# Asking for the next head's K six tiles earlier in an attention loop

## The chip, the cores and the metric

The kernel runs on one core of one Trainium2 chip. The metric is the device time of one execution in microseconds; the time before is the median of three runs. A separate, profiled execution gave the trace from which all durations here are taken.

## The reference

A transformer block with modulation: one attention over a given K and V cache, then a small mixer and MLP. B = 1, S = 2048, D = 640, 32 heads of 128, all tensors bf16.

```python
def _A_ref(x, k_cache, v_cache, wq, wo):
    q = (x @ wq).reshape(B, Sq, H, Dh).transpose(0, 2, 1, 3)
    scores = einsum('bhqd,bhkd->bhqk', q, k_cache) * Dh ** (-0.5)
    p = softmax(scores, axis=-1)
    o = einsum('bhqk,bhkd->bhqd', p, v_cache)
    return o.transpose(0, 2, 1, 3).reshape(B, Sq, H * Dh) @ wo
...
mod = (silu(c) @ w_mod)                      # sa, ca, ga, sb, cb, gb
h = layernorm(x) * (1 + ca) + sa
x = x + ga * _A_ref(h, k_cache, v_cache, wq, wo)
h = layernorm(x) * (1 + cb) + sb
return x + gb * _B_ref(h, w1, w2, w3, w4)    # shifted mixer and MLP
```

## The kernel before, in words

The kernel has three stages. The first loads x and the modulation weights, normalizes x and forms its transpose hT. The second, four fifths of the time, is attention. The third does the output projection, the mixer and the MLP.

**Attention** is one loop over steps s. Step s takes query tile j = s % 16 (128 queries) of head h = s // 16, so there are 512 tiles. For each tile:

1. TensorE computes the scores of 128 queries against 2048 keys into PSUM (qk, L297, tile Sps, in two halves of 1024 columns).
2. VectorE (DVE) reads each half once: it writes the scaled, negated scores to SBUF and takes the row minimum on the way (L570, tile negS). negS has three buffers, so DVE can be at most three tiles ahead of ScalarE.
3. GpSimd (POOL) joins the two minima (L580), and ScalarE (ACT) takes the exponential into one of eight buffers Pb (L583; eight RPB slots of the tile ring).
4. The probabilities must be transposed for the second product. For 15 of 16 tiles this is a transposing DMA from Pb to PTs, one of twelve RPT slots of the same tile ring (L234, "ring<-ring"). It is issued from SP, two tiles at a time: pairs (0,1), (2,3), (4,5), (6,7), (8,9), then tile 10 alone, then (12,13) and (14,15). Tile 11 is transposed by TensorE instead (t_piece, L264) and copied out by ACT (L273).
5. TensorE multiplies the transposed tile by V (pv, L310, tile PTp), eleven steps after the scores of that tile (PVD = 11; the lag falls to 8 in the last head). The product carries a column of ones, which gives the row sums. ACT copies it to Of (L561), POOL divides (L458) and stores four tiles at a time to a DRAM scratch tensor o_scratch (L465), on POOL's DMA queue.

Between these, TensorE computes the queries of head h+1 in pieces (q_piece, L248), which ACT copies out (L255).

**Loads.** K, transposed by the DMA on its way in (load_k, L207), and V (load_v, L226) have two buffers each, for even and odd heads. Heads 0 and 1 get their K ahead of the loop. At step j = 11 of a head (PVD) SP is given the K and the V of the next head, and in every fourth head a part of Wo (load_wo, L217). V can't be asked for earlier, since PV of the head before reads its buffer eleven steps behind the scores. K's buffer is read by qk only, and so is free once the last tile of the head before has its scores.

**Order.** Every engine runs its own list in the order in which the program adds operations, and waits for semaphores where an operation needs another engine's result. SP's list is a single queue too: a transposition waits on SP for the exponential of its second tile, and everything behind it on SP waits as well. K of head h+1 stands in SP's list behind the single transposition of tile 10, which stands behind that of tiles 8 and 9.

Of the kernel before, what the change touches and what calls it, by code (L numbers as in the profile page):

```python
# [115 lines left out]
def bass_adaLN_cond__mha_block_cached__mixer_s_mlp__prompt_kernel(  # L116
# [3 lines left out]
    _, H, SK, DH = A_k_cache.shape  # L120
# [17 lines left out]
    with ExitStack() as es:  # L138
# [11 lines left out]
        if True:  # L150
            with ExitStack() as es1:
# [53 lines left out]
                def load_k(h):  # L205
                    hb = h % 2
                    G.dma("sync", lambda e: e.dma_start_transpose(KTs[:, hb], A_k_cache[0, h]), ("k", hb), w=[("KT", hb)])  # L207
# [24 lines left out]
                def transpose(g, n):  # L232
                    b, t = g % RPB, g % RPT
                    G.dma("sync", lambda e: e.dma_start_transpose(  # L234
                        PTs[:, t:t + n].rearrange("p r k q -> p (r k) q"), ring[:, b:b + n].rearrange("p r s -> p (r s)")),
                        ("t", b), r=[("Pb", b + i) for i in range(n)], w=[("PT", t + i, z) for i in range(n) for z in range(2)])
# [9 lines left out]
                def q_piece(h, cc, q):  # L246
                    jb = bank(("q", h, cc))
                    G.op("tensor", lambda t: t.matmul(JB[jb], wqg[:, h // WG, q, (h % WG) * 128:(h % WG + 1) * 128], hT[:, q, cc * 512:(cc + 1) * 512],  # L248
                                                      start=(q == 0), stop=(q == KT - 1)),
                         r=[("wq", h), ("hT", cc, q)], w=[("J", jb)])  # L250
# [39 lines left out]
                def qk(s, half):  # L290
                    h, j = divmod(s, NQT)
                    hb = h % 2

                    def f(t):
                        for c2 in range(2):
                            col = half * 1024 + c2 * 512
                            ins = t.matmul(Sps[:, col:col + 512], QT[:, hb, j * 128:(j + 1) * 128],  # L297
                                           KTs[:, hb, col:col + 512], start=True, stop=True)
                        return ins
                    G.op("tensor", f, r=[("QT", hb, j // 4), ("KT", hb)],  # L300
                         w=[("S", half)] + ([("Sb", 2 * half), ("Sb", 2 * half + 1)] if s == 0 else []))
# [110 lines left out]
                def q_head0(cc):  # L412
                    for q in range(KT):
                        q_piece(0, cc, q)
                    q_evac(0, cc)
# [22 lines left out]
                def mod_rows(i):  # L438
                    n0, n1 = MROW[i]
                    bank = PO[:, (i % 2) * 512:(i % 2) * 512 + n1 - n0]  # L440

                    def f(t):
                        for k in range(KT):
                            ins = t.matmul(bank, s_bc[:, k, :], wmodr[:, k, n0:n1], start=(k == 0), stop=(k == KT - 1))
                        return ins
                    G.op("tensor", f, r=[("sbc", k) for k in range(KT)] + [("wm", 1)] + WRK, w=[("O", i % 2)])
                    G.op("scalar", lambda a: a.copy(mod_bc[:, n0:n1], bank), r=[("O", i % 2)], w=[("mod", i)])
# [79 lines left out]
                for s in range(at[-1] + LAG + 1):  # L527
                    h, j = divmod(s, NQT)
                    pvs = PVS.get(s, [])
                    evacs = []  # L530
                    if s <= 2:
                        for i in ((0,), (1, 2), range(3, len(MROW)))[s]:
                            mod_rows(i)
                    if s == 3:
                        G.op("gpsimd", lambda g: g.tensor_scalar(
                            out=mod_bc[:, 2 * D:3 * D], in0=mod_bc[:, 2 * D:3 * D], scalar1=1.0, scalar2=1.0, op0=ALU.add, op1=ALU.mult),
                            r=[("mod", i) for i in range(len(MROW))], w=["mod"])
                    for half in range(2):
                        if s < NG:
                            qk(s, half)  # L540
                        for g_ in pvs:
                            if len(pvs) == 1:
                                pv(g_, half)
                            elif g_ == pvs[half]:
                                pv(g_, 0)
                                pv(g_, 1)
                        if s == 0 and half == 1:
                            q_head0(NQC - 1)
                        if h + 1 < H and 2 * j + half in QPIECE:
                            cc, q = QPIECE[2 * j + half]  # L550
                            q_piece(h + 1, cc, q)
                            if q == KT - 1:
                                evacs.append((q_evac, h + 1, cc))
                        for r, pt in [(r, pt) for r in range(2) for pt in PE_TILES]:
                            g = s - PE_LAG[pt] - r
                            if 0 <= g < NG and g % NQT == pt:
                                t_piece(g, r, half)
                                if half == 1:
                                    evacs.append((t_evac, g, r))
                    for p in [g_ // 2 for g_ in pvs if g_ % 2 == 1]:  # L560
                        G.op("scalar", lambda a, p=p: a.copy(  # L561
                            Of[:, p % 4].rearrange("p z d -> p (z d)")[:, 0:259], PO[:, (p % 2) * 512:(p % 2) * 512 + 259]),
                            r=[("O", p % 2)], w=[("Of", p % 4)])
                    for fn, x, y in evacs:
                        if fn is q_evac or not by_dve(x, y):
                            fn(x, y)
                    for half in range(2):
                        if s < NG:
                            r8 = s % 8
                            G.op("vector", lambda v, half=half, s=s, r8=r8: v.tensor_scalar(  # L570
                                out=negS[:, s % 3, half * 1024:(half + 1) * 1024],
                                in0=Sps[:, half * 1024:(half + 1) * 1024],
                                scalar1=-SCALE, scalar2=None, op0=ALU.mult, op1=ALU.min,
                                accum_out=(nm0 if half == 0 else nm1)[:, r8:r8 + 1]),
                                r=[("S", half)], w=[("negS", s % 3), ("nmh", half, r8)])
                    for fn, x, y in evacs:
                        if fn is t_evac and by_dve(x, y):
                            fn(x, y)
                    if s < NG:
                        G.op("gpsimd", lambda g, r8=r8: g.tensor_scalar(  # L580
                            out=nm[:, r8:r8 + 1], in0=nm0[:, r8:r8 + 1], scalar1=nm1[:, r8:r8 + 1], scalar2=None, op0=ALU.min),
                            r=[("nmh", 0, r8), ("nmh", 1, r8)], w=[("nm", r8)])
                        G.op("scalar", lambda a, s=s, r8=r8: a.activation(  # L583
                            Pb[:, s % RPB, :], negS[:, s % 3, :], ACT.Exp, bias=nm[:, r8:r8 + 1], scale=-1.0),
                            r=[("negS", s % 3), ("nm", r8)], w=[("Pb", s % RPB)])
                        if not is_pe(s):
                            if s % 2 == 1 and not is_pe(s - 1):
                                transpose(s - 1, 2)
                            elif s % 2 == 1 or is_pe(s + 1):
                                transpose(s, 1)  # L590
                        if j == PVD:
                            if 1 <= h < H - 1:
                                load_k(h + 1)
                            if h < H - 1:
                                load_v(h + 1)
                            if h % WG == WG - 1:
                                load_wo(h // WG)
                    for g_ in NORMS.get(s, []):
                        gr, z = divmod(g_, 4)
                        if z == 0:  # L600
                            rcp(gr)
                        norm(gr, z)
                    if s == OT0:
                        load_ot(0)
                        for cc in range(NQC):
                            load_xt(cc)
                    if s == OT0 + 1:
                        load_ot(1)
# [247 lines left out]
```

## Time and profile before

| | |
|---|---|
| Median of 3 runs | 1690.23 us (1686.36 to 1691.68) |
| Profiled execution | 1699.03 us, span 1697.2 us |
| Attention, first DVE pass of head 0 to last of head 31 | 35.3 to 1343.9 us |
| One DVE pass over 1024 columns (L570) | 1220 ns, 1024 of them |
| One exponential over 2048 columns (L583) | about 2.0 us, 512 of them |
| Granted TensorE clock, mean | 0.962 of full |

On the profile's page, busy times are shares of the span for each engine, and the digits of section 2 are the busy tenths of 40 equal slices. The DMA row counts the core's 16 DMA engines together. SP's rows in a timeline are DMA issues: a row lasts from when SP begins to issue the transfer to when it is through with it, and the landing comes after. The other engines' rows are instructions; a bracket behind a row gives the idle time just before it and what ended that.

### The profile page before, as it was taken

What the parts mean: (1) busy time and instruction counts of PE and PEld (TensorE: products, weight loads), DVE (VectorE), ACT (ScalarE), POOL (GpSimd) and SP (SyncE); (2) the same over time, 40 slices, a digit from 0 to 9 for tenths busy, and PEclk for the clock granted to TensorE, in tenths of its full rate; (3) what the DMA queues carried; (4) which work ended last, traced back from release to release, by engine and by line L of the source; (5) the groups of instructions that cost most, each with busy time, mean ns of one, the idle gap of its engine ahead of it and who ended that gap; (6) DMA issues with size and microseconds to landing.
All of it is one profiled execution on the core that took longest, in us unless ns stands there. A gap on an engine that the chain in (4) does not pass through costs nothing.

```text
span 1697.2 us, 33782 instructions
## 1 busy us (share of the span) xinstructions
PE 1505.5 (89%) x13474; PEld 968.5 (57%) x13719; DVE 1376.4 (81%) x2428; ACT 1282.6 (76%) x1113; POOL 622.8 (37%) x1394
## 2 busy tenths in 40 slices
PE   5898978988989899889888888988989889999998
PEld 3466656655666566556555555656656645555444
DVE  6998978988999899889888888988989636666424
ACT  4999978988999899889898998888989700035330
POOL 0244434443444344434443444444434523332100
PEclk8999989999999999999999999999999999999999
DMA  9999999999999999999999999999999995620000
GB/s 304 234 239 242 236 224 225 241 237 234 247 234 236 242 243 236 230 222 240 231 240 232 233 230 233 235 229 227 245 243 223 241 249 110 140 103 3 13 20 32
DMA packets 1218285, 350.32 MB, mean 206 GB/s; under 512 B 1193744, under 2 KB 1212112, under 8 KB 1218128
## 3 DMA queue, kind: packets, MB, share of 16 engines
q1 hardware_dynamic: 1211984, 331.36, 97.7%
q0 software_dynamic: 6144, 16.79, 3.7%
q8 instruction: 108, 1.77, 0.4%
q14 instruction: 49, 0.40, 0.1%
HBM read 43.48 MB, written 19.40 MB: 37 GB/s over the span
## 4 chain that ended last, share of the span: by engine, by line
DVE 48%; PE 24%; DMA 11%; issue 8%; ACT 7%; SPq 2%; POOL 1%; POOLq 0%
DVE negS L570 47%; DMA kv<-in_A_k_cache_dram 8%; PE Sps L643 7%; ACT ring L583 5%; PE Sps L784 4%; PE Sps L297 3%; PE PTp L310 2%; PE Oaug L768 2%; PE QPp L768 2%; SPq L234 2%; PE Sps L753 1%; PE QPp L264 1%; DMA ring<-in_A_x_dram 1%; DVE ring L375 1%; DMA negS<-o_scratch 1%
## 5 line engine op out<-in xcount | busy, mean ns | idle before, releaser
L570 DVE TENSOR_SCALAR_CACHE_REDUCE negS<-Sps 128x1024 f32<-128x1024 f32 x1024 | 1177.8, 1220 | 132.2 <-PE Sps L297 129.9
L583 ACT ACTIVATE ring<-negS,small 128x2048 bf16<-128x2048 f32 x512 | 1021.2, 2005 | 37.5 <-POOL small L580 35.0
L297 PE MATMUL Sps<-kv 128*128 128x512 bf16 x1962 | 611.9, 391 | 148.8 <-DMA kv<-in_A_k_cache_dram 101.1
L310 PEld LDWEIGHTS PTp<-kv,ring 128*128 128x128 bf16 x8192 | 574.3, 100 | 256.5 <-issue 22.5
L310 PE MATMUL PTp<-kv,ring 128*128 128x129 bf16 x8192 | 661.3, 224 | 6.0 <-DMA ring<-ring 4.7
L580 POOL TENSOR_SCALAR small<-small 128x1 f32<-128x1 f32 x512 | 145.9, 285 | 715.6 <-DVE negS L570 715.6
L297 PEld LDWEIGHTS Sps<-kv 128*128 128x128 bf16 x2048 | 146.3, 99 | 274.9 <-DVE negS L570 131.7
L458 POOL TENSOR_SCALAR On<-Of,small 128x128 bf16<-128x128 f32 x512 | 189.8, 371 | 15.4 <-DMA o_scratch<-On 2.4
L561 ACT COPY Of<-PTp 128x259 f32<-128x259 f32 x256 | 92.3, 360 | 95.1 <-PE PTp L310 95.0
L681 ACT COPY kv<-PTp 128x640 bf16<-128x640 bf16 x32 | 22.0, 692 | 154.9 <-PE PTp L678 154.9
L451 POOL TENSOR_TENSOR small<-Of,small 128x4 f32<-128x4 f32 x128 | 133.1, 1040 | 5.0 <-ACT Of L561 4.9
L465 POOL DMA_DIRECT2D o_scratch<-On x128 | 103.1, 806 | 40.8 <-POOL On L458 37.2
L248 PE MATMUL Oaug<-hTx,wo 128*128 128x512 bf16 x258 | 98.0, 385 | 2.9 <-DVE hTx L407 2.9
L248 PE MATMUL QPp<-hTx,wo 128*128 128x512 bf16 x260 | 98.1, 382 | 2.8 <-ACT hTx L402 2.3
L570 DVE DVE_READ_ACCUMULATOR negS<-Sps 128x1 f32 x1024 | 84.7, 83 | 0.0
L624 POOL TENSOR_SCALAR On<-On 128x1 f32<-128x1 f32 x48 | 24.3, 507 | 151.7 <-DVE On L633 151.7
L651 DVE TENSOR_TENSOR ring<-Sps,mod_bc 128x640 f32<-128x640 f32 x16 | 13.2, 824 | 78.3 <-PE Sps L643 78.3
L643 PE MATMUL Sps<-wo,hTx 128*128 128x128 bf16 (+1 forms) x504 | 71.0, 302 | 6.0 <-DMA hTx<-o_scratch 5.6
L643 PE MATMUL Sps<-wo,negS 128*128 128x128 bf16 (+1 forms) x504 | 69.1, 298 | 1.1 <-DMA negS<-o_scratch 0.7
L788 DVE TENSOR_TENSOR ring<-Sps,ring 128x640 f32<-128x640 f32 x16 | 13.2, 824 | 66.2 <-PE Sps L784 66.2
L643 PEld LDWEIGHTS Sps<-wo,hTx 128*128 128x128 bf16 x512 | 40.0, 99 | 37.2 <-DMA hTx<-o_scratch 5.4
L643 PEld LDWEIGHTS Sps<-wo,negS 128*128 128x128 bf16 x512 | 39.5, 98 | 30.9 <-DMA negS<-o_scratch 0.6
(81 smaller groups left out, 906.8 us busy)
## 6 DMA issues: line engine op xcount, KB each, us to landing
kv<-in_A_v_cache_dram SPq DMA_DIRECT2D x32, 512.0 KB, 5.3
o_scratch<-On POOLq DMA_DIRECT2D x128, 128.0 KB, 5.0
ring<-in_A_x_dram SPq DMA_DIRECT2D x8, 640.0 KB, 4.9
wo<-in_A_wo_dram SPq DMA_DIRECT2D x8, 640.0 KB, 8.1
wo<-in_A_wq_dram SPq DMA_DIRECT2D x7, 640.0 KB, 8.5
ring<-ring SPq DMA_TRANSPOSE x256, 7.2
ring<-in_w_mod_dram SPq DMA_DIRECT2D x1, 3200.0 KB, 13.4
out_dram<-wo SPq DMA_DIRECT2D x16, 160.0 KB, 1.8
```

What stands on the lines that cost most here:

```text
L248: G.op("tensor", lambda t: t.matmul(JB[jb], wqg[:, h // WG, q, (h % WG) * 128:(h % WG + 1) * 128], hT[:, q, cc * 512:(cc + 1) * 512], star ...
L297: ins = t.matmul(Sps[:, col:col + 512], QT[:, hb, j * 128:(j + 1) * 128], KTs[:, hb, col:col + 512], start=True, stop=True)
L310: ins = t.matmul(ob[:, 0:129], PTs[:, b, kt, :], Vaug[:, hb, kt, 0:129], start=(kt == 0), stop=(kt == NKT - 1))
L451: G.op("gpsimd", lambda g: g.tensor_tensor(out=rl[:, 4 * b:4 * b + 4], in0=Of[:].rearrange("p a z d -> p (a z) d")[:, 4 * b:4 * b + 4, 128 ...
L458: G.op("gpsimd", lambda g: g.tensor_scalar(out=On[:, b, z, :], in0=Of[:, 2 * b + z // 2, z % 2, 0:128], scalar1=rl[:, 4 * b + z:4 * b + z ...
L465: G.dma("gpsimd", lambda e: e.dma_start(o_scr[jj // 2:jj // 2 + 2, :, hh].rearrange("a p z d -> p a (z d)"), On[:, b].rearrange("p (a z) d ...
L561: G.op("scalar", lambda a, p=p: a.copy(Of[:, p % 4].rearrange("p z d -> p (z d)")[:, 0:259], PO[:, (p % 2) * 512:(p % 2) * 512 + 259]), r= ...
L570: G.op("vector", lambda v, half=half, s=s, r8=r8: v.tensor_scalar(out=negS[:, s % 3, half * 1024:(half + 1) * 1024], in0=Sps[:, half * 102 ...
L580: G.op("gpsimd", lambda g, r8=r8: g.tensor_scalar(out=nm[:, r8:r8 + 1], in0=nm0[:, r8:r8 + 1], scalar1=nm1[:, r8:r8 + 1], scalar2=None, op ...
L583: G.op("scalar", lambda a, s=s, r8=r8: a.activation(Pb[:, s % RPB, :], negS[:, s % 3, :], ACT.Exp, bias=nm[:, r8:r8 + 1], scale=-1.0), r=[ ...
L643: ins = t.matmul(YB[b][:, c0:c0 + cw], OTj[pr % 2][:, 2 * hh + z, :], wo[:, hh, c0:c0 + cw], start=(hh == 0), stop=(hh == H - 1))
L768: ins = t.matmul(JB[jb][0:fsz[f_], :], w3[:, k, f_ * 128:f_ * 128 + fsz[f_]], nT[:, k, cc * 512:(cc + 1) * 512], start=(k == 0), stop=(k = ...
```

## The change

K of head h+1 is handed to SP at step j = 5, behind the transposition of tiles 4 and 5, in place of at step j = 11. Transpositions (6,7), (8,9) and (10) of the head now come after it in SP's list. V and Wo stay where they were. Which heads it holds for (1 to 30), and what is loaded, are the same.

```diff
                             elif s % 2 == 1 or is_pe(s + 1):
                                 transpose(s, 1)
+                        if j == 5 and 1 <= h < H - 1:
+                            load_k(h + 1)
                         if j == PVD:
-                            if 1 <= h < H - 1:
-                                load_k(h + 1)
                             if h < H - 1:
                                 load_v(h + 1)
                             if h % WG == WG - 1:
```

## The prediction

> **What bounds the kernel now.** I read the page first, then the waits of the attention stage, then SP's own timeline, because the page shows two things that are nearly always busy. The attention stage, slices 2 to 32, holds 80% of the span.
>
> ```profile
> span 1697.2 us, 33782 instructions
> PE 1505.5 (89%) x13474; PEld 968.5 (57%) x13719; DVE 1376.4 (81%) x2428; ACT 1282.6 (76%) x1113; POOL 622.8 (37%) x1394
> DMA  9999999999999999999999999999999995620000
> q1 hardware_dynamic: 1211984, 331.36, 97.7%
> ```
>
> The chain by line on the page says "DVE negS L570 47%", and a K wait 8%. One could stop there: DVE needs two passes of 1220 ns in a tile, one started every 1.145 us, so 2.29 us a tile and 36.7 us for 16 tiles. But a head takes longer: heads 1 to 30 run from 76.0 to 1306.3 us, 41.0 us each. The other 4.2 us a head (126 us in 30 heads, summed from gaps over 0.15 us between passes) are idle DVE, and the waits of that stretch name the reason:
>
> ```profile
> DVE negS L570 <- PE Sps L297: 124.4, 64, 7.4
> PE Sps L297 <- DMA kv<-in_A_k_cache_dram: 101.1, 29, 7.2
> ```
>
> So QK of a new head waits for K in 29 of 30 heads. The question is why K is late. SP's rows around the start of head 17 (first tile 272) show it. The first is the transposition of tiles 8 and 9 of head 16, then tile 10 alone, K, V, tiles 12/13, 14/15, and the first two pairs of head 17:
>
> ```profile
> 717.01 4.41 SPq L234 DMA_TRANSPOSE ring<-ring  x1
> 721.46 3.57 SPq L234 DMA_TRANSPOSE ring<-ring  x1
> 725.07 2.31 SPq L207 DMA_TRANSPOSE kv<-in_A_k_cache_dram  x1
> 727.43 0.58 SPq L226 DMA_DIRECT2D kv<-in_A_v_cache_dram  x1
> 728.05 5.45 SPq L234 DMA_TRANSPOSE ring<-ring  x1
> 733.55 4.31 SPq L234 DMA_TRANSPOSE ring<-ring  x1
> 739.80 4.20 SPq L234 DMA_TRANSPOSE ring<-ring  x1
> 744.46 4.37 SPq L234 DMA_TRANSPOSE ring<-ring  x1
> ```
>
> Each row starts 0.04 us after the one before it ends: SP is a full pipe. A pair takes 4.0 to 5.5 us of it and lands 2 to 3 us later. Beside these rows, what made the pairs ready, and what K held up:
>
> ```profile
> 710.10 3.92 ACT L583 ACTIVATE ring<-negS,small 128x2048 bf16<-128x2048 f32 x2
> 729.67 1.03 PE L297 MATMUL Sps<-kv 128*128 128x512 bf16 x2 [5.65 <-DMA kv<-in_A_k_cache_dram]
> 737.77 2.00 ACT L583 ACTIVATE ring<-negS,small 128x2048 bf16<-128x2048 f32 x1 [0.68 <-POOL small L580]
> ```
>
> Tiles 8 and 9 had their exp done at 714.0, and SP came to them at 717.0. So SP was 3 us behind, K had to stand behind that backlog, and was asked for 4.6 us before QK began. The profile's list of SP's waits puts hundreds of microseconds of L234 down to ACT; I don't follow it, since these pairs had been ready for microseconds. The one true wait is the hole from 737.86 to 739.80: the exp of head 17's second tile ends at 739.77, and its pair is issued 0.03 us later. SP ran dry there because head 17 had started late. The DMA engines feel it:
>
> ```profile
> core 0: us, PE busy (x) PEld busy (x) DVE busy (x) ACT busy (x) POOL busy (x), PEclk, DMA share, GB/s
> 737.00:738.00 1.00, 1.00 (x12) 0.75 (x11) 1.00 (x3) 0.32 (x2) 0.55 (x2) 1.00 1.21 279
> 738.00:739.00 1.00, 0.95 (x11) 0.68 (x11) 1.00 (x3) 1.00 (x1) 0.08 (x1) 1.00 0.88 199
> 739.00:740.00 1.00, 1.00 (x12) 0.73 (x11) 1.00 (x3) 1.00 (x2) 0.26 (x2) 1.00 0.00 0
> 740.00:741.00 1.00, 1.00 (x12) 0.70 (x11) 1.00 (x3) 0.97 (x2) 0.70 (x3) 1.00 0.00 1
> 741.00:742.00 1.00, 1.00 (x12) 0.71 (x11) 1.00 (x3) 1.00 (x2) 0.47 (x1) 1.00 1.19 274
> ```
>
> For two microseconds nothing moves. My reading: SP's queue with the DMA engines behind it is the bound, at about 40 us a head against DVE's 36.7. The K wait is how DVE is held back to it, and the only part of that wait that costs time is what empties the queue.
>
> **The change, part by part.** Nothing is added or removed: 30 K loads (for heads 2 to 31) move ahead of three transpositions, (6,7), (8,9) and (10). Three things follow.
>
> *K itself.* It needs its buffer, last read by QK of the head before, over when this head starts; it adds no wait on SP. It is asked for some 11 us earlier in queue time (4.29 + 4.76 + 2.02, the median rows of those three issues). The K wait goes.
>
> *What it is moved past.* The three go 2.2 us (K's median row) later. PV reads a tile 11 tiles (25.2 us) after its DVE pass; tile 8 of head 16 started on DVE at 706.6 and was landed at 723.0, 16.5 us. That cover holds, with 6 to 8 us to spare. V, Wo and (12,13) keep their place in the sum, and POOL's stores to o_scratch are not behind SP.
>
> *Where the stall goes.* Without the K wait DVE outruns the queue by 3 us a head until a buffer stops it: exp of tile s needs tile s-8's transposition landed (8 slots of Pb), and DVE may be three tiles ahead of exp. So the wait moves to exp L583 or to PV L310 on "ring<-ring", in small pieces, with several pairs always ready on SP. K keeps up at that limit: it lands 4.6 us after (4,5) are issued (725.07 to 729.62), while exp of 12 and 13 can start only when (4,5) land, 2.1 to 2.6 us after issue, and take 2.3 us each. The next head's first DVE pass needs tile 13's negS buffer, so comes 6.7 us or more after that issue. Margin: 2 us.
>
> The sum, against the profiled execution (1699.03 us, span 1697.2):
> - Holes in SP's queue in heads 1 to 30, from its rows: 27.4 us in all. 1.7 us lie at head 1's start, before any moved load can help. Left: 25.7 us, the upper bound if issue times stay.
> - From the other side: the 13 heads without a hole and without a Wo load hold 38.98 us of issues plus 0.4 us of hand-overs; the seven with Wo 42.6 plus 0.5. 23 x 39.4 + 7 x 43.1 = 1208 us against 1230.2: 22 us. I take this one, because it lets the dry heads (38.7 us of issues) cost what full ones do.
> - At the end SP waits 2.9 us (1355.1 to 1358.0) for the o_scratch store before the first load of the output projection. With DVE further ahead of SP that may vanish: 0 to 2.9, I take 2.
> - K's own issue: 1.79 to 3.18 us among its rows, 2.2 the median. In its new place it may meet other traffic: -12 to +29 us over 30 loads. I take 0, since it lies between transpositions in both places.
>
> Sum -24 us: 1675 for the profiled execution. That one ran 8.8 us above the median of the runs shown; from 1690.2 the forecast is 1666 us (-1.4%).
>
> **Rivals.**
> *The whole K wait is won.* If the queue isn't a bound, because its issues shrink when spread better, DVE sets the pace. The stage moves 235 GB/s over 1230 us, 9.64 MB a head; at the 279 GB/s of the row above that is 34.5 us, below DVE. Then up to 126 us go: 1565 to 1640 us. Against it: full heads issue no faster than dry ones. The Trainium skill ("DMA: Bandwidth & Descriptors", Latency and other measured facts) gives 261 GB/s for transposing DMAs with a non-contiguous middle dimension; as an estimate that is 36.9 us a head, no bound beside DVE. The trace differs from it both ways: 279 in a microsecond of transpositions alone, 235 with V and stores among them. Chance 0.11.
>
> *Nothing changes.* K between pairs costs 1 us more each (3.18 rather than 2.2), or full-time backlog stretches the issues as pairs stretch from 4.2 to 5.2-5.5 now and then. 30 x 0.8 = 24 us eats the gain: 1687 to 1693. The same result comes if K is still late after all, because the backlog grows past the buffers; the margin of 2 us speaks against that. Chance 0.11.
>
> *Slower, by the clock.* After the 5.65 us wait above TensorE's granted clock reads 0.50 at 733 us, and the next two tiles each leave DVE 0.9 us idle: 1.8 us for a cold spell, now at most one per head. If PV's waits for transpositions come as several long ones per head, a head costs 36.7 + 1.8n; n = 3 gives 42.1 against 41.0 now, +33 us, 1723. It decides above n = 2. Against it: waits for one pair are the difference between a pair's issue and 4.6 us of production, 1 to 2 us; only behind V and Wo do 6 to 9 us pass between landings. The Trainium skill ("TensorE: Matmul & The Clock Gate", HAM oscillation) lets the clock drop after idle gaps of more than about 3.4 us. The 5.65 us above agree with it. Chance 0.08.
>
> **How the numbers follow.** My case has 0.70. About 0.3% (5 us) is what can be told from no change. Faster: 0.70 + 0.11 = 0.81; same 0.11; slower 0.08. The range takes my case with its unknown costs and the no-change case. At the low end K's rows are at their shortest (12 us) and a dozen heads issue like the cheapest full head (37.5 us, 1.5 less each): 30 us lower, 1636. The high end is no change, 1692. Left out are the clock and nearly all of the big gain, 0.19 together.
>
> **What would show it.** Right: the K wait under 10 us in total; SP's rows without holes from head 3 on; new waits of ACT L583 or PE L310 on ring<-ring of 60 us or more; heads of about 40.2 us; DVE still idle about 3.5 us a head. Wrong: K waits remain (the move doesn't reach); heads near 37 us (the queue was no bound); K rows near 3 us; several stretches per head at clock 0.5.

## The result, and the profile after

The changed kernel takes 1681.31 us (median of 13 runs, 1674.12 to 1687.72) against 1691.68 us (13 runs, 1685.46 to 1702.92). The ratio is 0.9932, 95% interval 0.9911 to 0.9953: 11.5 us faster by the ratio (8 to 15). The forecast was 24 us, to 1666 us with a range of 1636 to 1692: the time lies in the range, and the gain is a little under half of the forecast. The traced run of the changed kernel took 1676.82 us.

From the page of the changed kernel: span, the DMA queue fed by SP, the chain by engine, and the groups of DVE's and ACT's main instructions (behind the second bar: idle time before them, and what ended it).

```profile
span 1675.0 us, 33782 instructions
q1 hardware_dynamic: 1211984, 331.36, 99.5%
DMA 30%; ACT 27%; PE 20%; DVE 15%; issue 6%; POOL 1%; SPq 0%; ACTq 0%; DVEq 0%; POOLq 0%
L570 DVE TENSOR_SCALAR_CACHE_REDUCE negS<-Sps 128x1024 f32<-128x1024 f32 x1024 | 1182.6, 1221 | 103.2 <-ACT ring L583 64.3
L583 ACT ACTIVATE ring<-negS,small 128x2048 bf16<-128x2048 f32 x512 | 1013.5, 2013 | 116.5 <-DMA ring<-ring 99.8
```

K is gone from the waits. In its place stand the two waits that the prediction named (us in total, times, longest):

```profile
ACT ring L583 <- DMA ring<-ring: 99.8, 62, 5.9
...
PE PTp L310 <- DMA ring<-ring: 23.0, 13, 6.3
```

SP's rows around the K of head 16 (whose first DVE pass is at 672.0 us): pair (4,5) of head 15, K, pairs (6,7) and (8,9), tile 10, then V and Wo (left out), and pair (12,13):

```profile
659.66 4.31 SPq L234 DMA_TRANSPOSE ring<-ring  x1
664.01 2.63 SPq L207 DMA_TRANSPOSE kv<-in_A_k_cache_dram  x1
666.69 5.72 SPq L234 DMA_TRANSPOSE ring<-ring  x1
672.45 4.37 SPq L234 DMA_TRANSPOSE ring<-ring  x1
676.87 1.66 SPq L234 DMA_TRANSPOSE ring<-ring  x1
...
680.64 7.68 SPq L234 DMA_TRANSPOSE ring<-ring  x1
```

SP's rows now follow each other almost without holes: heads 1 to 30 hold under 1 us of them, in three places. DVE starts head 16 while SP is still at tiles 8 and 9 of head 15, eight tiles back, which is the depth of Pb. ACT stands still where that depth ends:

```profile
675.14 2.00 ACT L583 ACTIVATE ring<-negS,small 128x2048 bf16<-128x2048 f32 x1 [4.06 <-DMA ring<-ring]
```

So the wait went where the forecast put it, and the size is off by half. The experiments ask two things: is SP's queue really the bound, and what became of the other 12 us.

For the second, one cut serves all runs: from the issue of head 1's first pair to the end of the last transposition's issue. That stretch is the sum of SP's rows (issues), of what the gaps between rows have beyond 0.06 us each (holes), and of the hand-overs that are left (14 to 16 us in the traces of the table). What comes before it and after it in the span is the same within 1.2 us each in all traces of the table. All numbers are us, from SP's rows. The expectations for e1 and e2 count heads 1 to 30 by another cut (1203 us of issues in the first trace); of those, only the comparison carries over to the table.

| trace | stretch | issues | holes |
|---|---|---|---|
| before (K at step 11) | 1271.0 | 1231.2 | 25.3 |
| e1, K at 11 | 1259.7 | 1221.9 | 23.2 |
| e11, K at 11 | 1270.6 | 1225.9 | 29.9 |
| after (K at 5) | 1248.4 | 1233.4 | 0.9 |
| e2, K at 5 | 1256.9 | 1241.9 | 1.0 |
| e8, K at 7 | 1250.0 | 1235.1 | 0.9 |
| e3, K at 9 | 1256.5 | 1240.8 | 1.7 |
| e5, K at 12 | 1366.3 | 1204.0 | 146.8 |

### The profile page after: what moved, and what is told of

It reads as the page before. It is cut to its first block, busy times and chain, and to the rows that moved or that the text cites. A ratio compares the mean times of both kernels' runs of the same rounds, so it can differ in the third digit from the quotient of the medians.

```text
span 1675.0 us, 33782 instructions
## 1 busy us (share of the span) xinstructions
PE 1496.1 (89%) x13474; PEld 945.3 (56%) x13719; DVE 1381.6 (82%) x2428; ACT 1264.6 (75%) x1113; POOL 625.5 (37%) x1394
## 4 chain that ended last, share of the span: by engine, by line
DMA 30%; ACT 27%; PE 20%; DVE 15%; issue 6%; POOL 1%; SPq 0%; ACTq 0%; DVEq 0%; POOLq 0%
DMA ring<-ring 28%; ACT ring L583 21%; DVE negS L570 14%; PE Sps L643 7%; PE Sps L784 4%; ACT ring L273 2%; PE Oaug L768 2%; PE QPp L768 2%; ACT Of L561 2%; ACT kv L255 2%; PE Sps L753 1%; PE Sps L297 1%; DMA ring<-in_A_x_dram 1%; PE PTp L310 1%; DVE ring L375 1%
## 5 line engine op out<-in xcount | busy, mean ns | idle before, releaser
L583 ACT ACTIVATE ring<-negS,small 128x2048 bf16<-128x2048 f32 x512 | 1013.5, 2013 | 116.5 <-DMA ring<-ring 99.8
L310 PEld LDWEIGHTS PTp<-kv,ring 128*128 128x128 bf16 x8192 | 566.0, 99 | 271.8 <-DMA ring<-ring 31.2
L310 PE MATMUL PTp<-kv,ring 128*128 128x129 bf16 x8192 | 653.5, 222 | 24.3 <-DMA ring<-ring 23.0
L297 PEld LDWEIGHTS Sps<-kv 128*128 128x128 bf16 x2048 | 137.8, 98 | 217.1 <-DVE negS L570 184.3
L248 PE MATMUL Oaug<-hTx,wo 128*128 128x512 bf16 x258 | 102.2, 401 | 21.4 <-ACT ring L273 18.4
L561 ACT COPY Of<-PTp 128x259 f32<-128x259 f32 x256 | 95.9, 374 | 12.1 <-PE PTp L310 12.1
L248 PEld LDWEIGHTS Oaug<-hTx,wo 128*128 128x128 bf16 x320 | 32.4, 101 | 48.4 <-ACT ring L273 34.0
```

The lines of the kernel that those rows point to most:

```text
L310: ins = t.matmul(ob[:, 0:129], PTs[:, b, kt, :], Vaug[:, hb, kt, 0:129], start=(kt == 0), stop=(kt == NKT - 1))
L561: G.op("scalar", lambda a, p=p: a.copy(Of[:, p % 4].rearrange("p z d -> p (z d)")[:, 0:259], PO[:, (p % 2) * 512:(p % 2) * 512 + 259]), r= ...
L583: G.op("scalar", lambda a, s=s, r8=r8: a.activation(Pb[:, s % RPB, :], negS[:, s % 3, :], ACT.Exp, bias=nm[:, r8:r8 + 1], scale=-1.0), r=[ ...
```

## The experiments

**Both kernels again** (e1, e2, and later e11 as a third trace of the kernel before). The edits are none, or the change undone.

> The kernel before once more, with a trace of its own. Theory Q (SP's queue of DMA issues is the bound; the early K only fills the holes that the K wait leaves in it; the forecast of 24 us was read from one trace whose run, at 1699 us, was longer than the typical run of 1691): time 1690 us; holes in SP's queue in heads 1 to 30 clearly under the 27 us of the first trace, 8 to 20 us, with the issues themselves again near 1203 us in sum. Rival S (the holes are always about 27 us, and half of what they free is lost again because issues get longer in a queue that is always full): holes 24 to 30 us again.

> The changed kernel once more, with a trace of its own. Theory Q: 1680 us, 0.993 of before; holes under 4 us in heads 1 to 30; issues in sum 1195 to 1210 us, no more than before's. Rival S: holes under 4 us too, but issues in sum 10 us or more above those of the kernel before.

> A third trace of the kernel before. Rival S: holes 22 to 27 us again, issues in sum from head 1's first pair to the last 1215 to 1232 us, below the 1233 to 1242 us of the four traces without holes. Theory Q: issues in sum as in those four.

e1: 1693.34 us, ratio 1.0013 (0.9993 to 1.0034). e2: 1682.45 us, ratio 0.9957 (0.9935 to 0.998). e11: one run, 1700.24 us. The expectation that the first trace's 27 us of holes were an unlucky draw fell: the three traces of the kernel before have 25.3, 23.2 and 29.9. e11's 29.9 is above the 22 to 27 that rival S had given. The issues speak for the rival S: 1226 us on average with K at 11, 1238 in the four traces with next to no holes, each of the four above each of the three. Single traces of one kernel lie 8 to 9 us apart, so one pair of traces could not show this; the first pair has 1231.2 and 1233.4.

**K in other places.** e3 and e8 ask for K at steps 9 and 7, e5 at step 12, behind V:

```diff
-                        if j == 5 and 1 <= h < H - 1:
+                        if j == 9 and 1 <= h < H - 1:      # e3; j == 7 in e8
                             load_k(h + 1)
```
```diff
                                 load_wo(h // WG)
+                        if j == 12 and 1 <= h < H - 1:     # e5
+                            load_k(h + 1)
```

> K asked for at step 9, behind tiles 8 and 9 and ahead of tile 10 alone: one issue of 2.0 us earlier than in the kernel before, and two pairs later than in the changed kernel. Theory Q: the K wait on TensorE falls from 101 us by about 2 us a head to 40 to 55 us, most holes go (4 to 12 us left), time within 4 us of the changed kernel: 1680 to 1686 us. Theory D (DVE sets the pace, every microsecond of K wait costs time): half the K wait left means half the gain, 1686 us, and holes play no part. Rival S: as D in time, with issues longer than before's.

> K at step 7, between steps 5 and 9. Theory Q and rival S both: no holes (under 4 us), K wait under 40 us, time equal to K at 5 and at 9, 1679 to 1684 us. It is one more trace of a queue without holes: S expects its issues in sum above 1235 us from head 1's first pair to the last, Q no more than the 1222 to 1231 us of the traces with K at 11.

> The other direction: K asked for at step 12, behind V (and Wo) in place of ahead of them, some 3 us later than in the kernel before. The K wait and the holes behind it should grow by up to 2 to 3 us a head, 40 to 80 us of holes in all. Theory Q (a microsecond of hole costs a microsecond, issues keep their length): time grows by as much as the holes, 1710 to 1745 us. Rival S (part of each hole comes back, because issues beside holes are shorter): holes grow as much, the sum of the issues falls below the 1222 to 1231 us of the two traces of the kernel before (from head 1's first pair to the last), and the time grows by half to three quarters of the holes: 1700 to 1725 us.

e3: 1680.1 us, ratio 0.9937 (0.9912 to 0.9962), the same as with K at 5. But its K wait is nearly whole:

```profile
PE Sps L297 <- DMA kv<-in_A_k_cache_dram: 87.7, 26, 6.9
```

The expected 40 to 55 us missed. This is the plainest answer to "what did the K wait cost": 88 of 101 us are still waited, and the gain is complete, because the holes are down from 26 to 1.7 us. It also shows that the gain is not one of TensorE's clock: the mean grant in e3's trace is 0.968, near the 0.962 of before, where K at 5 has 0.980. A head that waits for K loses nothing as long as SP has something to issue. e8 lies between: 1680.81 us, 59.4 us of K wait, where under 40 had been expected, and no holes.

e5: 1795.47 us, ratio 1.060 (1.056 to 1.0639). Both theories missed the size, because K's row behind V takes 4.46 us on average (133.9 us for 30) in place of 2.36, so K is late by that too:

```profile
683.76 0.58 SPq L226 DMA_DIRECT2D kv<-in_A_v_cache_dram  x1
684.38 3.83 SPq L207 DMA_TRANSPOSE kv<-in_A_k_cache_dram  x1
```

This is no new work in the queue. The row that follows V (or V and Wo) is a long one: in the other traces of the table it is that of the pair (12,13), and in e5 those pairs take 137 us for 30 heads in place of 202 with K at 11. K's rows grow by 63 us and theirs shrink by 65. The K wait nearly doubles:

```profile
PE Sps L297 <- DMA kv<-in_A_k_cache_dram: 176.0, 30, 7.8
```

The split is what matters. Against K at 11 the holes grow by 121 us and the issues as a whole shrink by 22, so 0.18 us of each microsecond of hole comes back in shorter issues. The rival had a quarter to a half; the direction is the rival's.

**The queue's load.** e4 leaves the K loads of heads 2 to 31 out; those heads work with the K of heads 0 and 1. e6 and e7 have TensorE transpose tile 10 as well, with K at 5 and at 11; e10 moves one of the copies to VectorE.

```diff
-                        if j == 5 and 1 <= h < H - 1:       # e4
-                            load_k(h + 1)
```
```diff
-                PE_TILES = (11,)
+                PE_TILES = (10, 11)                         # e6, e7, e10
-                by_dve = lambda g, r: False
+                by_dve = lambda g, r: g % NQT == 10 and r == 0   # e10 alone
```

> The K loads of heads 2 to 31 are left out altogether: those heads use the K of heads 0 and 1. No head waits for K, and 30 issues of 2.2 us are gone from SP's queue. Theory Q: each head gets shorter by K's own 2.2 us: 66 us less than the changed kernel, about 1615 us (limit: DVE's 36.7 us a head, 1577 us). Theory D (the queue isn't a bound once K is early): within 10 us of the changed kernel, 1671 to 1681 us.

> K at step 5, and TensorE transposes tile 10 too (tiles 10 and 11 in place of 11 alone). That takes one single transposition of 2.0 to 2.3 us out of SP's queue in each head and gives ScalarE two more copies of 1 us, TensorE 16 more small transposes. Theory Q: the queue falls to 38 us a head, ScalarE at 37.1 + 2 = 39 us becomes the next bound; 1 us a head or more is won over the changed kernel: 1630 to 1655 us. If ScalarE or TensorE binds harder than its busy time says: no change or slower, 1680 us or more.

> Tiles 10 and 11 on TensorE, and K at step 11 as in the kernel before. Theory Q: the backlog ahead of K is shorter by the single of tile 10, so the K wait falls to 40 us or less, but the queue is no longer the only bound and holes cost less; time within 10 us of the same kernel with the early K. If the K wait is what costs: 20 us or more above it.

> K at step 5, tiles 10 and 11 on TensorE, and one of the four copies out of PSUM (tile 10, first half) on VectorE in place of ScalarE. ScalarE leads the chain with two tiles on TensorE (47% of it). Theory Q with ScalarE as next bound: ScalarE falls by 1 us a head, VectorE rises by 1 to 37.7; up to 25 us less than with both copies on ScalarE, 1590 to 1612 us. If VectorE's extra pass lies on the path: no change or slower, 1615 us or more.

e4: 1595.21 us, ratio 0.945 (0.9425 to 0.9474): 86 us less than the changed kernel. Thirty K issues of 2.37 us are 71 us, so more than the whole of their own time was won, although no head waits for K in the changed kernel either; the issues of the transpositions are 14 us shorter as well (1120.5 us against 1134.7). So the bound is SP's queue with the transfers behind it. Whether SP's issuing or the DMA engines set the length of a row, these runs do not separate. DVE now leads the chain:

```profile
DVE 30%; ACT 25%; PE 21%; DMA 14%; issue 10%; SPq 0%; POOL 0%; ACTq 0%; DVEq 0%; POOLq 0%
```

e6: 1614.72 us, ratio 0.9539 (0.9497 to 0.958), better than expected (1630 to 1655) and, with e10, the fastest of the kernels that compute everything, 4.6% under the kernel before. One single less per head in SP's queue brought 67 us over the changed kernel. ScalarE leads the chain there, as expected:

```profile
ACT 47%; PE 23%; DVE 13%; issue 13%; DMA 3%; POOL 1%; SPq 0%; DVEq 0%; POOLq 0%; ACTq 0%
```

e7: 1631.7 us, ratio 0.9638 (0.9594 to 0.9682), 17 us above e6, between the two expectations (within 10, or 20 and more). Its K wait is 40.3 us, at the edge of what was expected, and its holes are 65 us against 15 in e6. e10: 1615.15 us, ratio 0.9509 (0.9462 to 0.9556). The expected 1590 to 1612 us missed, and the interval overlaps that of e6, so no gain over e6 is shown. (e9, e10 and e11 ran on another chip, where the kernel before has a median of 1695.49 us against 1691.08 for e5 to e8; compare them by their ratios.) Taking 1 us a head off ScalarE filled e6's remaining 15 us of holes (1.2 left), and the issues grew from 1154.6 to 1173.6 us in these two traces. With one trace each that is no proof, but it is the same pattern as in the table. An extra pass of VectorE on the path, the rival in the expectation, isn't excluded.

**Why the issues grow.** The traces show stalls of the transposing packets: 256-byte packets that take over 40 ns in place of 18. In the four traces with next to no holes, 48 to 49% of these slow packets lie in the 2.5 us after the start of an instruction fetch, which is 26% of the time (last section). e9 leaves out half of PV, eight of the sixteen products of a tile, and so 8192 of TensorE's instructions:

```diff
-                        for kt in range(half * 8, half * 8 + 8):
+                        for kt in range(half * 8, half * 8 + 4):
-                                           start=(kt == 0), stop=(kt == NKT - 1))
+                                           start=(kt == 0), stop=(kt == 11))
```

> K at step 5. Half of PV is left out: of the 16 products per tile the last four of each half are not computed, so the program has 8192 TensorE instructions fewer; every transposition, load and store stays. In the traces so far, 108 of the 131 instruction fetches (8 to 16 KB each) between head 1's first pair and the last coincide with a stall of the transposing packets of about 1.4 us, 145 to 170 us in all. Theory F (the fetches cause these stalls, in a queue that is the bound): a quarter of the fetches goes, some 95 to 100 are left, issues in sum fall by 30 to 50 us below the 1233 to 1242 us of the other traces with a full queue, time 1630 to 1655 us. Rival (the stalls only happen to lie there, or TensorE's own time counts): with TensorE no bound, no change, 1676 to 1686 us.

e9: 1661.1 us, ratio 0.979 (0.9741 to 0.9838), against 0.9932 to 0.9957 for the changed kernel. By these ratios 24 to 28 us are won by cutting instructions of an engine that isn't the bound, with every load, store and transposition kept:

```profile
span 1667.1 us, 25835 instructions
PE 1379.9 (83%) x9623; PEld 698.2 (42%) x9623; DVE 1381.8 (83%) x2428; ACT 1263.9 (76%) x1113; POOL 622.7 (37%) x1394
```

Fetches fall from 131 to 99; all 32 that go are of 16 KB (88 to 56). Those followed within 2.5 us by at least 20 slow packets fall from 114 to 120 in the four full queues to 85. Issues are 1224.9 us, 13 below the four, in a traced run that was the longest of its four (1668.88). Theory F expected 30 to 50 us: the direction came, the size did not. One reason can be read from SP's rows: a pair in whose row a 16 KB fetch starts takes 5.08 to 5.13 us in the four traces, a pair without a fetch 4.32 to 4.36 (pairs behind loads and holes left out). That is 0.7 to 0.8 us for a fetch and not 1.4, and 32 of them would be some 24 us. The edit also halves TensorE's reads of PTs and V, and the runs don't separate that from the fetches.

## Why the prediction was right or wrong

- **The queue is the bound: right.** e4 and e6 show it, and e3 shows that the K wait itself costs nothing once SP has work. One detail of the reading is off: of the rows shown, the last starts 0.46 us after the one before it, so there is a second, small hole that the text passes over.
- **K needs no new wait, and its margin holds: right.** The list of waits of the changed kernel has no K in it.
- **Where the stall goes: right.** 99.8 us at exp and 23.0 at PV, on transpositions; DVE idle 93 us in heads 1 to 30 (3.1 a head, 3.5 forecast); heads of 40.1 us (40.2 forecast). The last agreement is partly luck: 40.1 is measured between DVE's first passes, and DVE gains a lead on the queue in these heads that doesn't shorten the span. Between SP's first pairs a head takes 40.35 us in this trace and 40.5 on average in the four with next to no holes, against 40.95 in the three with K at 11.
- **The holes, 22 to 26 us: right.** 26.1 on average before, 1.1 in a queue with early K: 25 us freed.
- **"The dry heads cost what full ones do": wrong, and this is the term that halved the gain.** It stood for issues that keep their length once the holes are filled, and allowed 0.3 us for each dry head alone. Measured, the sum of issues grows by 11.5 us (1226.3 to 1237.8, averages of three and four traces). All of it is in the transpositions (L234: 1123.6 to 1134.7); K's rows make 71 us in both. The 0.3 us also hung on where a head is cut. The prediction's 38.98 and 38.7 come out if a head is cut at its pair (14,15); with the 23 heads without Wo cut at the other seven rows of the same trace, the ten with the largest holes are 0.2 to 1.9 us cheaper than the rest. So the first trace left this term open between 2 and 19 us, and the sum took a value near the low end. (A hole can also come from short rows before it, so no cut gives a clean price.) A part of the growth is seen directly: in the three traces with K at 11, a pair issued behind a hole of over 0.3 us takes 4.37 to 4.40 us, other pairs 4.56 to 4.59 (pairs behind V or Wo left out). At 29 to 39 such pairs in a trace that is 5 to 7 us. e5's 0.18 us per microsecond of hole gives 4.5 us for 25. The rest, some 5 or 6 us, agrees with more fetches that meet a stall (106 to 113 in the three traces with holes, 114 to 120 in the four without, at 0.7 to 0.8 us each). That it is only this is argued, not shown, and that part of the cause stays open.
- **The end, 2 us: wrong, 0.** What follows the last transposition is 342.1 to 343.3 us in the traces with K at 11 and 342.1 to 342.7 in the four with K earlier. SP's row for the first load of the output projection starts right behind the row before it in both first traces and lasts 8.14 us before and 8.25 after.
- **K's own issue, 0: right on average** (2.36 us a load with K at 11, 2.37 in the four traces without holes).
- The account: 25.0 of holes and 0.6 of hand-overs, less 11.5 of longer issues, are 14 us between the traces; the timed medians have 10 to 12. The traced runs of the kernel before (1699.0, 1689.5, 1700.2) lie 4 us above its median on average, which covers the difference. Making the sum against a run 9 us above the median did little harm; taking the price of a full queue from one trace and one cut did.
- **The rivals.** "The whole K wait is won" fell with the result itself, and e3 shows why. "Nothing changes" named the right danger, longer issues in a full queue, at 24 us where 11.5 came. "Slower, by the clock" did not come: the mean grant rose from 0.962 to 0.980.

## What to carry to other kernels

A wait costs only what it takes from the resource that is the bound: before pricing a wait, look whether that resource runs dry during it, and count the holes there, not the waiting engine's idle time. And don't assume that a queue runs at the same rate when it is kept full: here 11.5 of the 25 us of holes came back as longer issues, and in e5 0.18 us for each microsecond. Get that part from repeated traces or from a variant with larger holes, not from one trace. Taking a transfer out of the queue that is the bound (e6, 67 us for one tile in sixteen) was worth far more here than reordering it.

## What the runs showed of the hardware

The transposing DMA stalls where instructions are fetched. In the changed kernel's trace, a fetch of 16 KB starts at 655.87 us and lasts 1.03 us on its DMA engine. The windows around it, with DMA share and GB/s in the last two columns:

```profile
core 0: us, PE busy (x) PEld busy (x) DVE busy (x) ACT busy (x) POOL busy (x), PEclk, DMA share, GB/s
655.00:656.00 1.00, 1.00 (x12) 0.72 (x11) 1.00 (x1) 1.00 (x2) 0.60 (x2) 1.00 1.28 279
656.00:657.00 1.00, 1.00 (x12) 0.61 (x10) 1.00 (x3) 1.00 (x1) 0.65 (x2) 1.00 2.26 155
657.00:658.00 1.00, 1.00 (x12) 0.57 (x10) 1.00 (x3) 1.00 (x3) 0.00 (x0) 1.00 0.18 37
658.00:659.00 1.00, 0.93 (x11) 0.58 (x10) 1.00 (x3) 0.92 (x2) 0.51 (x2) 1.00 1.27 290
```

SP was in the middle of a row then (654.85, 4.77 us), so the queue was not dry. Averaged over the 78 fetches of 16 KB between 100 and 1200 us of this trace, the transposing packets start at 900 to 960 per us before a fetch and at under 80 per us from 1.0 to 1.75 us after its start; 2 us after it they are back at 880, and then run at 1010 to 1060 for a while, so a part is made up. The loss is about 1.3 to 1.4 us in the first 2 us of a fetch, and 0.7 to 0.8 us in the length of the pair's row on SP. Fetches of 8 KB lengthen that row by 0 to 0.3 us in the four traces with next to no holes.

The Trainium skill ("Runtime: NRT & Kernel Launch", Instruction fetch mechanics) has fetches come in 16 KiB blocks, with a cost that is mostly hidden. The size agrees with 88 of the 131 fetches in the stretch of the table; the other 43 have 8 KB. Hidden the cost is not, where the queue of transpositions is the bound: its packets stop, as above. e9, with 32 fewer fetches, was faster, as this would have it, but it also left out half of PV, so it is no proof of the cause.
